# Attention scores by halves of their rows, q's norms by a diagonal and ones, single-row first tiles, first products of block 0 by kc

## The chip, the cores and the metric

The kernel runs on one core of a Trainium2 chip. The core has TensorE (PE, with its weight loads shown as PEld), VectorE (DVE), ScalarE (ACT), GpSimd (POOL) and SyncE (SP), each with a queue of its own that is worked off in order; DMA transfers are issued from the queues of SP and ACT. The metric is device time in microseconds, the median of several runs.

## What is computed

With N = 6016 tokens and C = 256 channels (B = 1); `moe_w_in` is 256 x 2048, `moe_w_out` 2048 x 256, and the second layer has the same shapes:

```python
qn = q / (np.linalg.norm(q, axis=1, keepdims=True) + 1e-06)
kn = k / (np.linalg.norm(k, axis=1, keepdims=True) + 1e-06)
s = kn.transpose(0, 2, 1) @ qn / tau          # 256 x 256
a = np.exp(s - s.max(-1, keepdims=True))
a /= a.sum(-1, keepdims=True) + 1e-09
x = v @ a
h = x @ w_in;   x = (h / (1 + np.exp(-1.702 * h))) @ w_out
h = x @ w2_in;  x = np.maximum(0.01 * h, h) @ w2_out
```

The weights come as float64 and are converted on the chip.

## The kernel before

**Front.** q and k are read in 15 tiles of 1, 1, 2, ten times 4, 2 and 1 rows of 128 tokens (`rows`, L318). `load_qk` issues q's transfer on SP and k's on ACT for the first three tiles and on SP after that, eight tiles ahead (`AHEAD`). For each tile PE forms the scores (L382): two products per row (kc = 0, 1), q's half as weights, k's row as moving operand, in full float32, so that each product is two instructions in the trace; all of them add up in two banks of PSUM (`s_ps`). ACT squares each tile and DVE adds the squares into `acc` (`add_squares`). Ahead of the last two tiles' scores PE forms the column sums of `acc` (`norms`, four products by `ones`, eight instructions). DVE and ACT make from them 1 / (norm + 1e-6); `dq` is a diagonal matrix of q's inverse norms over tau, `rk` holds k's as a scalar per row. ACT copies the scores to `st` (L436), four products by the diagonal (L442) scale them and bring them to the other orientation, and DVE takes each row's maximum (L450) for ACT's exponential (L455), which also adds up the denominators `den`. Four transposes (L463) turn the exponentials; `eth` and `etl` are their high and low parts (a float32 rounded to the one-pass format fp32r, and the rest).

**Splitting.** Every large product after the scores is three fp32r products, high by high, high by low and low by high (`terms`, L92). `halves` makes the two parts: a cast on ACT (L95) and a subtraction on DVE (L96).

**Fold.** Since x = v @ a is only used as x @ w_in, the attention is folded into the first weights: `fold(f)` multiplies `eth`/`etl` by the converted weight `wi` f (12 products of 256 columns), ACT scales by the denominators into `raw` (L490), DVE splits it into `wa[f]` (L496) and `raw` is stored to `w1raw[f]`. Fold 0 is made in the front, fold 1 within the hidden products of `f == NF`, the others in the loop over f.

**Block 0.** v's first 1024 tokens (two columns of blocks, u = 0, 1) are loaded into the buffer of q and k tile `V_TILE`, transposed by PE (`transpose_v`, eight transposes for each u, L410) and split into `xa[0]` (kc = 0) and `xbt` (kc = 1). For each of 8 weight tiles f and both halves s of the hidden units, `hidden_first` forms the hidden products of both u (12 instructions of 512 columns), ACT applies the gelu into `h` (one buffer, L514) and casts it to `gd` (L680), and DVE subtracts. `pend` holds finished hidden tiles; `emit_y(len(pend) - 2)` forms the output products y of the tiles before the last two, so y always lags one hidden tile behind.

**Weights.** `jobs` is a generator of small steps that convert a weight from float64: a scaling on ACT (L182), three integer steps on DVE (L203, L208, L212), a cast and a subtraction on DVE. `go_on(n)` puts the next n steps at the place where it is called; `next_load` issues the load of another weight on SP, at most three at a time. The order of weights is wi 0, wo 0, wi 1, wi 2, wo 1 and so on. The steps are called with 5 behind the scores of the second to last tile, 2, 2 and 4 in the rest of the front, and 4 and 2 in turn in block 0.

The rest of the kernel (blocks 1 to 5 of both layers, by seven products instead of eight) isn't touched. Within each engine, instructions run in the order in which the program emits them.

## Time and profile before

| | us |
|---|---|
| median of 3 runs (lowest, highest) | 1041.66 (1041.51, 1043.06) |
| the profiled execution | 1043.86 |
| its span | 1042.0 |
| PE busy | 1031.5 (99%) |
| DVE busy | 775.0 (74%) |
| ACT busy | 589.9 (57%) |

A page sums up one profiled execution. Its orders of time list, per engine, when a run of like instructions began, how long it lasted until the modelled end of the last, how many there were, and in brackets how long the engine had stood idle before and whom it then waited for. The granted clock is 1.00 at 2.4 GHz and 0.50 at 1.2 GHz.

### The profile page before, as it was taken

How to read it: one execution, taken by the hardware profiler on the slowest of the kernel's cores; microseconds unless marked ns; L12 is line 12 of the kernel's file. 1: busy time of each engine (PE TensorE's matmuls, PEld its weight loads, DVE VectorE, ACT ScalarE, POOL GpSimd, SP SyncE). 2: the span in 40 equal slices, each digit the busy share in tenths (PEclk: the TensorE clock that was granted, in tenths of full speed). 3: DMA queues.
4: the chain of work that ended last, by engine and by line, in shares of the span. 5: the costliest groups of instructions: out<-in, count | busy, mean ns of one | idle time of the engine just before them, and what ended most of it. 6: DMA issues, size and time to landing. Idle time of an engine off the chain costs nothing.

```text
span 1042.0 us, 12633 instructions
## 1 busy us (share of the span) xinstructions
PE 1031.5 (99%) x4676; PEld 870.6 (84%) x4676; DVE 775.0 (74%) x1187; ACT 589.9 (57%) x864; POOL 0.7 (0%) x7
## 2 busy tenths in 40 slices
PE   8999999999999999999999999999999999999998
PEld 7878888888888888888998888888888888888997
DVE  6889868888888888888766667577567667676655
ACT  5465555666556666666556555555555555455453
POOL 0000000000000000000000000000000000000000
PEclk9999999999999999999999999999999999999999
DMA  9646423015224223212744002101200300300202
GB/s 361 234 126 167 129 65 91 10 31 150 92 68 110 98 76 103 89 56 96 263 167 152 1 1 42 41 1 19 63 1 9 73 1 1 76 1 1 41 1 36
DMA packets 120077, 81.82 MB, mean 79 GB/s; under 512 B 93392, under 2 KB 104400, under 8 KB 118736
## 3 DMA queue, kind: packets, MB, share of 16 engines
q1 hardware_dynamic: 115872, 80.04, 25.3%
q10 hardware_dynamic: 4144, 0.98, 0.4%
q8 instruction: 36, 0.59, 0.2%
q14 instruction: 25, 0.20, 0.1%
HBM read 55.05 MB, written 25.95 MB: 78 GB/s over the span
## 4 chain that ended last, share of the span: by engine, by line
PE 97%; DVE 1%; DMA 1%; issue 0%; ACT 0%; ACTq 0%; DVEq 0%
PE y L92 49%; PE h L92 44%; PE y L382 4%; DMA qk<-in_k_dram 1%; DVE gd L99 0%; PE h L442 0%; ACTq L330 0%; ACT raw L490 0%; ACT sc L455 0%; DVE ta L208 0%; PE h L357 0%; DVE ta L203 0%; DVE etl L99 0%; DVE eth L467 0%; DVE ta L212 0%
## 5 line engine op out<-in xcount | busy, mean ns | idle before, releaser
L92 PE MATMUL y<-gd,wo 128*128 128x512 f32 (+1 forms) x1248 | 296.5, 386 | 0.1
L92 PE MATMUL h<-xa,wa 128*128 128x512 f32 (+1 forms) x1152 | 276.5, 385 | 0.5 <-DVE wa L496 0.5
L92 PEld LDWEIGHTS y<-gd,wo 128*128 128x128 f32 x1248 | 233.8, 188 | 44.1 <-DVE gd L99 0.4
L92 PEld LDWEIGHTS h<-xa,wa 128*128 128x128 f32 x1152 | 216.2, 188 | 41.7 <-DVE wa L496 0.8
L92 PE MATMUL y<-g,wo 128*128 128x512 f32 (+1 forms) x1044 | 246.8, 385 | 0.0
L92 PEld LDWEIGHTS y<-g,wo 128*128 128x128 f32 x1044 | 196.0, 188 | 36.3
L92 PE MATMUL h<-xb,wa 128*128 128x512 f32 (+1 forms) x888 | 217.3, 385 | 0.0
L92 PEld LDWEIGHTS h<-xb,wa 128*128 128x128 f32 x888 | 166.7, 188 | 31.1
L99 DVE TENSOR_TENSOR tv<-tp,h 128x512 f32<-128x512 f32 (+1 forms) x88 | 59.3, 674 | 114.4 <-PE h L92 111.8
L99 DVE TENSOR_TENSOR cc<-tv,h 128x512 f32<-128x512 f32 (+1 forms) x176 | 116.0, 673 | 34.9 <-PE h L92 34.4
L96 DVE TENSOR_TENSOR gd<-cc,gd 128x1024 fp32r<-128x1024 f32 (+1 forms) x87 | 104.1, 1197 | 0.0
L722 ACT COPY tp<-h 128x512 f32<-128x512 f32 (+1 forms) x87 | 50.4, 580 | 93.2 <-PE h L92 92.6
L95 ACT CAST gd<-cc 128x1024 fp32r<-128x1024 f32 (+1 forms) x87 | 90.0, 1035 | 0.0
L516 ACT ACTIVATE cc<-cc 128x1024 f32<-128x1024 f32 (+2 forms) x49 | 50.3, 1027 | 38.9 <-DVE cc L99 38.9
L516 ACT ACTIVATE tt<-tt 128x512 f32<-128x512 f32 (+1 forms) x48 | 30.0, 625 | 72.4 <-DVE tt L99 72.4
L99 DVE TENSOR_TENSOR tt<-tv,h 128x512 f32<-128x512 f32 (+1 forms) x88 | 59.4, 675 | 9.9 <-DVE tv L99 0.9
L99 DVE TENSOR_TENSOR tt<-tt,h 128x512 f32<-128x512 f32 (+1 forms) x88 | 59.4, 675 | 9.2
L514 ACT ACTIVATE cc<-cc 128x1024 f32<-128x1024 f32 (+1 forms) x40 | 41.6, 1041 | 40.9 <-DVE cc L99 40.9
L99 DVE TENSOR_TENSOR g<-tt,g 128x512 fp32r<-128x512 f32 (+1 forms) x87 | 58.6, 673 | 7.2 <-ACT g L733 6.9
L514 ACT ACTIVATE tt<-tt 128x512 f32<-128x512 f32 (+1 forms) x40 | 24.9, 623 | 64.8 <-DVE tt L99 64.8
L99 DVE TENSOR_TENSOR g<-tp,g 128x512 fp32r<-128x512 f32 (+1 forms) x87 | 58.6, 674 | 0.0
L746 ACT CAST g<-tp 128x512 fp32r<-128x512 f32 (+1 forms) x87 | 53.2, 612 | 2.8
(97 smaller groups left out, 713.0 us busy)
## 6 DMA issues: line engine op xcount, KB each, us to landing
cv<-in_moe_w_in_dram SPq DMA_DIRECT2D x32, 256.0 KB, 3.2
cv<-in_moe_w_out_dram SPq DMA_DIRECT2D x16, 512.0 KB, 3.9
wa<-w2a SPq DMA_DIRECT2D x8, 896.0 KB, 4.7
qk<-in_q_dram SPq DMA_DIRECT2D x10, 512.0 KB, 9.9
qk<-in_k_dram SPq DMA_DIRECT2D x10, 512.0 KB, 10.0
x<-stg SPq DMA_DIRECT2D x5, 1024.0 KB, 4.6
stg<-x SPq DMA_DIRECT2D x5, 1024.0 KB, 5.2
out_dram<-o SPq DMA_DIRECT2D x80, 64.0 KB, 1.9
```

The source lines that it names most:

```text
L92: nc.tensor.matmul(dst, lhsT=w, rhs=x, start=start, stop=stop, skip_group_check=more)
L95: nc.scalar.copy(hi, raw)
L96: nc.vector.tensor_tensor(out=lo, in0=raw, in1=hi.bitcast(F32), op=ALU.subtract)
L99: nc.vector.tensor_tensor(out=out, in0=in0, in1=in1, op=op)
L382: nc.tensor.matmul(s_ps[kc][:, :C], lhsT=t[:, 0, r, kc * P:(kc + 1) * P], rhs=t[:, 1, r, :], start=(j == 0 and r == 0), stop=(j == last an ...
L514: nc.scalar.activation(out=out, in_=in_, func=AF.Gelu_apprx_sigmoid)
L516: nc.scalar.activation(out=out, in_=in_, func=AF.Prelu, alpha=0.01)
L722: nc.scalar.copy(tp, pa)
L746: nc.scalar.copy(g11[:, 0], tp)
```

## The change

- The first tiles are six single rows, then 2, nine times 4, 2 and 1; k's loads of the first four go on ACT's queue. `ones` becomes 128 x 128 and is set before `ident`; the warm-up products use it.
- In the scores k's half is now the weight and q's row the moving operand, so that `s_ps[h]` holds 128 rows of k's channels by 256 of q's. For the last four tiles (11 rows) only half 0 is formed in the loop; half 1's 22 instructions are spread over what follows (`second_half`).
- The squares of the last three tiles are made for q and k apart, and the norms come behind all of half 0's scores.
- `st` and the four products by the diagonal go. `spread` multiplies the diagonal by `ones`, which gives q's inverse norms on every partition; ACT copies them to `rq`, and one `tensor_tensor_reduce` on DVE scales a half's scores and takes the row maxima.
- Softmax, turning, splitting and fold 0 are each done for one half h (or one kc) at a time, in an order written out by hand among transposes of v, scores and the kc = 0 part of the first hidden products (`first_products`).
- The casts of the high parts of `eth`, wi 0, wi 1 and wo 0 go from DVE to ACT.
- `V_TILE` becomes 10; one weight is loaded ahead of v and two behind it. The conversion steps in the front are 4, 1 and 5.
- For f = 0 the subtraction comes ahead of the four conversion steps, y of half s = 0 is not formed before the hidden products of s = 1, fold 1 comes between y of s = 0 and y of s = 1, and `pend` is emptied there.

`turn(h)` makes two transposes of `ex[:, h]` into bank h3; `fold_products` and `fold_scale` are the old loops of `fold` for one kc, with the high parts of `eth` first. Core of the diff:

```diff
-    ones = small(const, 1, "ones")
+    ones = const.tile([P, P], F32, name="ones")
...
+        nc.gpsimd.memset(ones, 1.0)
         make_identity(nc, ident)
-        nc.gpsimd.memset(ones, 1.0)
...
                 hi, lo = (wo[f][:, s].rearrange("p k c -> p (k c)") for s in range(2))
-                nc.vector.tensor_copy(hi, flat)
+                (nc.scalar.copy if f == 0 else nc.vector.tensor_copy)(hi, flat)
...
-                nc.vector.tensor_copy(wi[:, 0], flat)
+                (nc.scalar.copy if f < 2 else nc.vector.tensor_copy)(wi[:, 0], flat)
...
-        rows = [1, 1, 2] + [4] * 10 + [2, 1]
+        rows = [1] * 6 + [2] + [4] * 9 + [2, 1]
...
-                eng = nc.scalar if j < 3 and i == 1 else nc.sync
+                eng = nc.scalar if j < 4 and i == 1 else nc.sync
...
-        V_TILE = 7
-        CONVERT = {last - 1: 5}
+        V_TILE = 10
+        LATE = last - 3
...
+        def squares(j, i):
             t, n = qk(j), rows[j]
             sq = front.tile([P, 2, 4, C], F32, tag="sq", name="sq", bufs=2)
+            nc.scalar.activation(out=sq[:, i, :n, :], in_=t[:, i, :n, :], func=AF.Square)
+            for r in range(0, n, 2):
+                m = min(2, n - r)
+                add(acc[:, i, :m, :], acc[:, i, :m, :], sq[:, i, r:r + m, :])
+        def scores(j, halves_of, some=None):
+            t, n = qk(j), rows[j]
+            for r in range(n) if some is None else some:
+                for h in halves_of:
+                    nc.tensor.matmul(
+                        s_ps[h][:, :C],
+                        lhsT=t[:, 1, r, h * P:(h + 1) * P],
+                        rhs=t[:, 0, r, :],
+                        start=(j == 0 and r == 0),
+                        stop=(j == last and r == n - 1),
+                    )
...
+            scores(j, range(KC) if j < LATE else (0,))
...
             if j == V_TILE:
-                for _ in range(3):
-                    next_load()
+                next_load()
                 nc.sync.dma_start(out=taub, in_=tau.partition_broadcast(P))
                 for c in range(2):
                     nc.sync.dma_start(
                         out=qk(V_TILE)[:, c],
                         in_=v[c * BLK:(c + 1) * BLK, :].rearrange("(t p) c -> p t c", p=P),
                     )
+                for _ in range(2):
+                    next_load()
+        for j in range(LATE + 1, last + 1):
+            for i in range(2):
+                squares(j, i)
+        add(acc[:, :, 0, :], acc[:, :, 0, :], acc[:, :, 1, :])
+        for j in range(LATE + 1, last + 1):
+            scores(j, (0,))
+        go_on(4)
+        norms()
...
-        for d in range(KC):
-            nc.scalar.copy(st[:, d, :], s_ps[d][:, :C])
-        go_on(2)
-        sq_ps = [bank("h2"), bank("h3")]
-        for kc in range(KC):
-            for d in range(KC):
-                nc.tensor.matmul(
-                    sq_ps[kc][:, d * P:(d + 1) * P],
-                    lhsT=st[:, d, kc * P:(kc + 1) * P], rhs=dq[:, d, :], start=True, stop=True,
-                )
-        vt0 = transpose_v(0, ("y01", "y11"))
+        def spread():
+            nc.tensor.matmul(
+                nrm[:, C:2 * C], lhsT=ones, rhs=dq.rearrange("p k c -> p (k c)"),
+                start=True, stop=True,
+            )
+            nc.scalar.copy(rq, nrm[:, C:2 * C])
+        vt = {}
+        def transpose_v(kc, tags):
+            for u, tag in enumerate(tags):
+                vt[kc, u] = bank(tag)
+                for i in range(BLK // P):
+                    nc.tensor.transpose(
+                        vt[kc, u][:, i * P:(i + 1) * P],
+                        qk(V_TILE)[:, u, i, kc * P:(kc + 1) * P], ident,
+                    )
+        def split_v(kc, u):
+            dst = xbt if kc else xa[0]
+            halves(dst[:, 0, u], dst[:, 1, u], vt[kc, u])
+        def softmax(h):
+            nc.vector.tensor_tensor_reduce(
+                out=sc[:, h], in0=s_ps[h][:, :C], in1=rq, scale=rk[:, h:h + 1],
+                scalar=-3.0e38, op0=ALU.mult, op1=ALU.max, accum_out=mx[:, h:h + 1],
+            )
             nc.vector.tensor_scalar(
+                out=nmx[:, h:h + 1], in0=mx[:, h:h + 1], scalar1=-1.0, scalar2=None, op0=ALU.mult
             )
             nc.scalar.activation(
+                out=ex[:, h], in_=sc[:, h], func=AF.Exp, bias=nmx[:, h:h + 1],
+                scale=1.0, accum_out=den[:, h:h + 1],
             )
+        def split_e(h):
+            cols = slice(h * P, (h + 1) * P)
+            src = et[:, h * C:(h + 1) * C].rearrange("p (d c) -> p d c", d=KC)
+            nc.scalar.copy(eth[:, :, cols], src)
+            subtract(etl[:, :, cols], src, eth[:, :, cols].bitcast(F32))
+            nc.vector.tensor_scalar_add(rden[:, h:h + 1], den[:, h:h + 1], 1e-9)
+            nc.vector.reciprocal(out=rden[:, h:h + 1], in_=rden[:, h:h + 1])
...
+        def fold_half(raw, f, kc):
+            at = slice(0, 4, 3) if kc == 0 else slice(1, 3)
+            hi, lo = wa[f][:, 0, at], wa[f][:, 1, at]
+            nc.vector.tensor_copy(hi, raw[:, at])
+            subtract(lo, raw[:, at], hi.bitcast(F32))
+        late_rows = [(j, r) for j in range(LATE, last + 1) for r in range(rows[j])]
+        def second_half(count):
+            for j, r in late_rows[:count]:
+                scores(j, (1,), (r,))
+            del late_rows[:count]
+        transpose_v(0, ("h1", "h2"))
+        split_v(0, 0)
+        second_half(2)
+        spread()
+        go_on(1)
+        softmax(0)
+        split_v(0, 1)
+        second_half(4)
+        et = bank("h3")
+        turn(0)
+        split_e(0)
+        second_half(3)
+        wi0 = ready.pop(0)
+        raw0 = early.tile([P, 4, P], F32, tag="tp", name="raw")
+        pw0 = [bank(tag)[:, :C] for tag in ("y01", "y11")]
+        fold_products(pw0[0], wi0, 0)
+        second_half(len(late_rows))
+        transpose_v(1, ("y00", "h1"))
+        softmax(1)
+        fold_scale(raw0, pw0[0], 0)
+        fold_half(raw0, 0, 0)
+        hp0 = {}
+        def first_products(kc, pairs):
+            for s, u in pairs:
+                if kc == 0:
+                    hp0[s, u] = bank(f"h{2 * s + u}")
+                at = ((A11, A12), (A21, A22))[s][kc]
+                x = xbt if kc else xa[0]
+                terms(hp0[s, u], (wa[0][:, 0, at], wa[0][:, 1, at]), (x[:, 0, u], x[:, 1, u]),
+                      kc == 0, kc == KC - 1)
+        first_products(0, [(0, 0)])
+        turn(1)
+        split_e(1)
+        split_v(1, 0)
+        first_products(0, [(1, 0)])
+        fold_products(pw0[1], wi0, 1)
+        fold_scale(raw0, pw0[1], 1)
+        split_v(1, 1)
         nc.scalar.preload_act_table(AF.Gelu_apprx_sigmoid)
+        fold_half(raw0, 0, 1)
+        nc.sync.dma_start(out=w1raw[0], in_=raw0)
+        first_products(0, [(0, 1), (1, 1)])
+        go_on(5)
...
-                hp = bank(f"h{2 * s + u}")
-                for kc, x in enumerate((xa[0], xbt)):
-                    terms(hp, (wa[g][:, 0, at[kc]], wa[g][:, 1, at[kc]]),
-                          (x[:, 0, u], x[:, 1, u]), kc == 0, kc == KC - 1)
+                if g == 0:
+                    hp = hp0[s, u]
+                    first_products(1, [(s, u)])
+                else:
+                    hp = bank(f"h{2 * s + u}")
+                    for kc, x in enumerate((xa[0], xbt)):
+                        terms(hp, (wa[g][:, 0, at[kc]], wa[g][:, 1, at[kc]]),
+                              (x[:, 0, u], x[:, 1, u]), kc == 0, kc == KC - 1)
                 act(1, h[:, u], hp)
-            if f == NF:
-                fold(1)
             nc.scalar.copy(gd[:, 0], h)
-            if f < 2 * NF - 1:
+            if 0 < g and f < 2 * NF - 1:
                 go_on(4)
             subtract(gd[:, 1], h, gd[:, 0].bitcast(F32))
+            if g == 0:
+                go_on(4)
             for u in range(2):
                 pend.append((1, 0, u, f, gd[:, 0, u], gd[:, 1, u]))
@@ -698,7 +769,15 @@
                         go_on(1)
                     if f:
                         fold(f + 1)
-                emit_y(len(pend) - 2)
+                if f == 0 and s == 0:
+                    continue
+                if f == 0:
+                    emit_y(2)
+                    fold(1)
+                    emit_y(2)
+                    fetch()
+                else:
+                    emit_y(len(pend) - 2)
                 if f + 1 < NF or s == 0:
                     go_on(2)
                 fetch()
```

## Rows read from the trace of the kernel before

**Rows 1.** The page, its first part: busy time of each engine.
```profile
PE 1031.5 (99%) x4676; PEld 870.6 (84%) x4676; DVE 775.0 (74%) x1187; ACT 589.9 (57%) x864; POOL 0.7 (0%) x7
```

**Rows 2.** Order of time of PE (with PEld): start, length, instruction, [idle before, releaser].
```profile
1.35 2.93 PE L372 MATMUL h<-ident 128*128 128x128 f32 x12 [1.35 <-POOL ones L132]
4.07 2.53 PE L382 MATMUL y<-qk 128*128 128x256 f32 x8
8.85 38.16 PE L382 MATMUL y<-qk 128*128 128x256 f32 x168 [2.25 <-DMA qk<-in_k_dram]
46.84 0.95 PE L357 MATMUL h<-ones,acc 128*128 128x1 f32 x8
47.65 2.84 PE L382 MATMUL y<-qk 128*128 128x256 f32 x12
50.51 1.37 PE L442 MATMUL h<-dq,st 128*128 128x128 f32 x8
51.72 1.04 PE L410 MATMUL y<-ident,qk 128*128 128x128 f32 x8
52.95 1.02 PE L463 MATMUL h<-ident,sc 128*128 128x128 f32 x4 [0.20 <-ACT sc L455]
54.75 0.50 PE L92 MATMUL h<-wi,eth 128*128 128x256 f32 x2 [0.78 <-DVE eth L467]
...
58.32 1.22 PE L92 MATMUL h<-xa,wa 128*128 128x512 f32 x3 [0.52 <-DVE wa L496]
...
66.09 2.40 PEld L92 LDWEIGHTS y<-gd,wo 128*128 128x128 f32 x11 [0.41 <-DVE gd L99]
...
75.75 0.84 PE L92 MATMUL h<-xa,wa 128*128 128x512 f32 x3
```

**Rows 3.** Windows, the scores (L382) alone: PE busy, instructions, granted clock, DMA share, GB/s.
```profile
9.00:10.00 1.00, 1.00 (x3) 0.50 1.03 418
...
12.00:13.00 1.00, 1.00 (x6) 0.91 1.04 426
...
15.00:45.00 30.00, 30.00 (x141) 1.00 0.89 339
```

**Rows 4.** DMA issues by size (to landing), and a window with its GB/s at the end.
```profile
qk<-in_q_dram SPq DMA_DIRECT2D x3, 128.0 KB, 2.7
...
qk<-in_k_dram ACTq DMA_DIRECT2D x1, 256.0 KB, 7.1
...
3.00:3.50 0.50, 0.50 (x4) 0.50 (x4) 0.00 (x0) 0.49 (x2) 0.00 (x0) 1.00 1.34 359
```

**Rows 5.** Order of time of all engines: the last additions of 4-row squares.
```profile
33.90 5.07 DVE L99 TENSOR_TENSOR acc<-acc,sq 128x1024 f32<-128x1024 f32 x4
```

**Rows 6.** Order of time of DVE and ACT from the conversion to the first y.
```profile
42.46 0.69 DVE L208 SCALAR_TENSOR_TENSOR ta<-cv,ta 128x512 int32<-128x512 int32 x1
...
47.82 0.16 DVE L417 TENSOR_SCALAR rr<-h 128x4 f32<-128x4 f32 x1 [2.68 <-PE h L357]
...
49.15 0.60 DVE L427 TENSOR_SCALAR dq<-ident,rn,rtau 128x128 f32<-128x128 f32 x2
...
51.47 0.43 DVE L450 TENSOR_REDUCE mx<-h 128x1 f32<-128x256 f32 x1 [0.58 <-PE h L442]
...
52.24 0.56 ACT L455 ACTIVATE sc<-h,mx,rk 128x256 f32<-128x256 f32 x1 [1.35 <-DVE mx L451]
...
53.94 0.57 ACT L95 CAST xa<-y 128x512 fp32r<-128x512 f32 x1
...
55.02 1.28 ACT L473 ACT_TABLE_LOAD   x1
...
56.97 0.84 ACT L490 ACTIVATE raw<-h,rden 128x256 f32<-128x256 f32 x2 [0.67 <-PE h L92]
...
62.28 1.05 ACT L680 CAST gd<-h 128x1024 fp32r<-128x1024 f32 x1
...
64.82 1.22 DVE L99 TENSOR_TENSOR gd<-h,gd 128x1024 fp32r<-128x1024 f32 x1
```

More of the change, by code (lines that the diff above doesn't have):

```diff
@@ L371, in tile_kernel @@
         for _ in range(6):
[L372 to L373 removed]
+            nc.tensor.matmul(warm[:, :P], lhsT=ones, rhs=ones, start=True, stop=True)
+        for j in range(LATE + 1):
             t, n = qk(j), rows[j]
[L375 to L391 removed]
+            scores(j, range(KC) if j < LATE else (0,))
+            sq = front.tile([P, 2, 4, C], F32, tag="sq", name="sq", bufs=2)
+            nc.scalar.activation(out=sq[:, :, :n, :], in_=t[:, :, :n, :], func=AF.Square)
+            for r in range(0, n, 2):
+                m = min(2, n - r)
+                add(acc[:, :, :m, :], acc[:, :, :m, :], sq[:, :, r:r + m, :])
             if j + AHEAD <= last:
@@ new lines, in fold_products, with fold_scale @@
+        def fold_products(pw, f_wi, kc):
+            c0 = slice(kc * P, (kc + 1) * P)
+            wi = f_wi.rearrange("p h (d n) -> p h d n", d=KC)
+            todo = [(eth, 0, d) for d in range(KC)] + [(eth, 1, d) for d in range(KC)]
+            todo += [(etl, 0, d) for d in range(KC)]
+            for i, (e, x, d) in enumerate(todo):
+                nc.tensor.matmul(
+                    pw, lhsT=e[:, d, c0], rhs=wi[:, x, d], start=i == 0, stop=i == len(todo) - 1
+                )
+        def fold_scale(raw, pw, kc):
+            nc.scalar.activation(
+                out=raw[:, 0::3] if kc == 0 else raw[:, 1:3],
+                in_=pw.rearrange("p (s n) -> p s n", s=2), func=AF.Copy,
+                scale=rden[:, kc:kc + 1],
+            )
@@ L481, in fold @@
             pw = bank("h0" if f == 1 else "h3").rearrange("p (k n) -> p k n", k=KC)
             for kc in range(KC):
[L483 to L486 removed]
+                fold_products(pw[:, kc], wi, kc)
             raw = early.tile([P, 4, P], F32, tag="tp", name="raw")
             for kc in range(KC):
[L490 to L494 removed]
+                fold_scale(raw, pw[:, kc], kc)
@@ L498, in fold @@
             nc.sync.dma_start(out=w1raw[f], in_=raw)
-        fold(0)
-        vt1 = transpose_v(1, ("y00", "y10"))
-        for dst, src in ((xa[0], vt1[0]), (xbt, vt1[1])):
-            halves(dst[:, 0, 1], dst[:, 1, 1], src)
-        go_on(4)
         fctx.close()
```

85 lines of the change are left out of this document (11 added, 74 removed).

## Prediction

> **What bounds the kernel now.** I read the page's head first: PE is busy for 99% of the span, DVE for 74% [rows 1]. A change to the front can therefore gain only what PE waits for there, or does there and need not do. Next I read PE's order of time over the first 76 us [rows 2]. The reader is to see three things. The six warm-up products and the first two tiles of scores run from 1.35 to 6.60; then PE stands 2.25 us for tile 2's k; and the following 168 score instructions run without a break. The clock's windows [rows 3] show what the stop costs beyond itself: from 9 to 10 the granted clock is 0.50 (the 1.2 GHz level), from 12 to 13 it is 0.91 on the way back to 2.4 GHz, and from 15 to 45 there are 141 instructions in 30 us, 0.213 each. So some 3.3 us at half pace lost 1.65 more.
>
> Behind the scores come small stops: 0.20 before the turning of the exponentials and about 0.5 inside it (four transposes last 1.02, eight of v last 1.04), 0.78 before the fold, 0.52 before the first hidden product and 0.38 inside it (1.22 for three, 0.84 at 75.75), 0.41 before the first y [rows 2]. Taken together: from the norms (46.84) to 75.75, where y of both halves of block 0, fold 1, hidden 1 and fold 2 are done, 28.9 us pass. Their instructions at dense pace are 12 score instructions x 0.213, norms 0.81, diagonal 1.2, 20 transposes x 0.115, 36 fold products x 0.12 and 60 products of 512 columns x 0.227 (from 0.84 for three, of which one lasts 0.386): 24.8. So 4.1 us of stops. Behind 75.75 PE is dense; that part only moves.
>
> **Part 1, the six single-row tiles.** Now tile 2 brings two rows by two transfers of 256 KB, the k of which lands 7.1 us after its issue; single-row transfers of 128 KB land after 2.7 [rows 4]. After, rows 0 to 5 come singly, the k of the first four on ACT's queue; while such small packets moved, 359 GB/s were carried [rows 4], which is 0.73 us a row against the 0.85 that PE needs for its four instructions. With row 0 landed by 3.4, row 4 is there at 6.3, row 5 at 7.1, the 2-row tile at 8.5 and the first 4-row tile, at the 426 GB/s of the window from 12 to 13 [rows 3], at 11. PE: the `ones` are set before the identity, so the warm-up starts some 0.4 earlier and tile 0 at 3.6; its four instructions go at half pace (1.7), because the eight of now take 2.53 where 0.213 each would be 1.7 [rows 2]; then 162 at 0.213. That is 3.6 + 1.7 + 34.5 = 39.8, and 0.3 for one late tile: 166 instructions by 40.1. The present kernel has 176 by 46.84, so 166 by 44.7. Term 1 is **-4.6**. Ends: -5.0 with no tile late; -2.3 if a stop like today's 2.25 comes back at the 4-row tile.
>
> The rule that speaks against this stands in the Trainium skill, "DMA: Bandwidth & Descriptors", section "Rules for kernel authors": at least 1 MiB a transfer for full bandwidth, and many small ones put together. Rows agree in kind (359 GB/s against 426) but not in what matters here, landing time.
>
> The norms need the squares too. DVE adds four rows in 2 x 1.27 [rows 5]. Tile 7 can be added from some 13.0 (landed at 11, squared by ACT first), eight 4-row tiles take it to 33.6, and the late tiles, now squared q and k apart, add 2.4 + 1.2 + 0.7 and the merge 0.7: 38.7. PE comes later, so no term; but DVE then has the first weight's three steps (1.8, by 0.69 [rows 6]) to do in front of the norms' first step, and is done with them at 40.5: no slack is left.
>
> Moved in SP's queue: v's two loads now stand ahead of the loads of wo 0 and wi 1, not behind them. v is first needed behind the norms, and lands sooner; wo 0 and wi 1 land later by v's 1 MB, 2.4 us at that rate, and are first wanted by ACT's scaling behind the norms. Loads and their users lie some 5 us apart, so I cost both at nothing; if that cover is gone, the stops at the first y grow by what is missing. The store of `raw` 0 comes later and is read only when all the first weights are folded: nothing.
>
> **Part 2, the order behind the norms.** Removed: `st` copies and four products by the diagonal (eight instructions, 1.2). Added: one product of `ones` by it (two, 0.43). Term 2 is **-0.75**. The ten score instructions that move behind the norms cost the same there; what counts is whether this work covers the chains. I walk the four queues in issue order from the norms' end (R), with durations of rows 6. Steps without a row are set as follows. `tensor_tensor_reduce` on 256 elements: the reduction that it replaces takes 0.43, and a second pass for the multiplication would make it 0.86; it reads the same columns, so a gain is excluded; I take 0.5, near the reduction, and the other end puts 0.36 on each half's chain. Half casts and half scalings: 0.3 to 0.42 (`raw`: 0.84 for two).
> - `spread` waits for dq: 1.93 from rr to dq, 0.16 behind DVE's other work; cover is eight transposes and four score instructions. Stop 0.45.
> - turn of half 0: copy 0.42, DVE still in v's and the weight's subtractions, then 0.5 + 0.2, exponential and its sum 0.7; cover eight score instructions (1.7). Stop 1.0.
> - first hidden product: half 1's scores end at R + 8.4, then 0.5, 0.2, 0.7, `fold_scale` 0.42, cast 0.3; cover only eight transposes. Stop 1.5.
> - second pair of first products: its bank h1 is held by v's transposes until `split_v(1, 1)` is through, whose ACT cast is queued behind `fold_scale(1)`, which waits for the fold. Stop 1.9.
> - first y: ACT has the table load (1.28), a scaling and the cast of wo 0, which waits for three DVE steps, queued in front of the activations of the hidden products (0.6 each), the 1024-wide cast (1.05) and DVE's subtraction (1.22). Today a fold and hidden products for the other half lie between; now half of these are done already. Stops 1.1 and 1.0.
> - fold 1: wi 1's cast waits on ACT and DVE, 0.7. y of the other half is now issued at once: its activations wait for that cast and for the first subtraction (one buffer `h`), 0.9. Hidden 1: 0.4.
>
> Sum 9.0 against 4.1: term 3 is **+4.9**. Ends: if ACT's casts of the weights are out of the way in time, the last stops (1.1, 1.0, 0.7, 0.9) vanish and the sum is 5.3, so +1.2; if the thin stretch brings the 1.2 GHz level again, +1.7 more, so +6.6.
>
> **Sum.** -4.6 - 0.75 + 4.9 = -0.45. DVE and ACT do nearly the same work in the later stages, which therefore take as long. The profiled execution has a span of 1042.0 and 1043.86 in all; the median of the runs is 1041.66. I put the difference on the median: **1041.2**. The half-pace stretch of this execution need not be in each run of before; where it is absent, term 1 is smaller by up to 1.65.
>
> **The rivals.**
> (a) Cover holds: faster. The front's gain stays and ACT is ahead of the casts; the stops are 5.3 to 6. -4.6 - 0.75 + 1.2 to 1.9 = -3.5 to -4.2: 1037.5. For it: ACT is busy for 57% [rows 1], and the loads may be there early. Against it: the casts wait for DVE, not for ACT's time. It decides if PE stops for less than 1 us at the first y. Chance 0.31.
> (b) The thin stretch slows the clock: slower. Between the turn of half 1 and the first y, PE would have stops of 1.9, 1.1 and 1.0 with some 3 us of work among them. Today a stop of 2.25 behind a short run of work was followed by 0.50 [rows 2, 3]; the stops of 0.2 to 0.8 around 53 were not. It decides where a stop of some 2 us follows others: +1.7, and with term 1 at -3.5 the sum is +2.3: 1044.0. Chance 0.14.
> (c) The loads don't come earlier: the 4-row tile lands late and the stop of 2.25 comes back, with or without the half pace. Term 1 is -2.3, or less, and the sum +1.9 or more: 1043.8. The page's rule on small transfers would bring it out so. Chance 0.10.
> (d) My forecast, within 0.2%: 0.45.
>
> **How the numbers follow.** The bound of 0.2% (2.1 us) is about what a measurement of this kernel can tell from no change. Faster is (a), 0.31; slower is (b) and (c), 0.24; the rest 0.45. The low end takes -5.0, -0.75 and +1.2: -4.5, 1037.2. The high end takes -2.3, -0.75 and +6.6: +3.5, 1045.2; I cut it to 1044.6, since (b) and (c) together are rare. The forecast's own range is 1039.6 to 1043.7.
>
> **What would show it.** Part 1: no PE stop over 1 us before the norms, weight loads at full pace from some 5 us on, norms at 39.5 to 41. Wrong if a wait on `qk` over 1 us stands there. Part 2: stops in the places and sizes above, named by the chain's rows `ex`, `raw`, `xb`, `gd`; wrong if the first y starts under 20 us after the norms' end (rival a), or if the clock's column shows 0.5 between 45 and 70 (rival b). Later: PE dense from about 72, and phases of equal length.

## The result, and the profile after

| | before | after |
|---|---|---|
| median of 4 runs (lowest, highest), us | 1042.2 (1041.51, 1043.06) | 1048.23 (1046.98, 1049.48) |
| the profiled execution | 1043.86 | 1046.98 |
| its span | 1042.0 | 1045.2 |

The ratio after to before is 1.0057, with an interval of 1.004 to 1.0075: the changed kernel is slower by 6.0 us, outside the range that I gave. Each run also lists its span and the mean granted clock of that span. Where this mean is 0.999 or 1.0, which I call "at full clock" from here on, the medians of one kernel's spans lie close together: 1040.15 to 1040.3 for before in four series (its single runs from 1039.0 to 1041.1), 1045.2 and 1045.6 for after. The other two runs of after, at 0.998, have 1047.3 and 1047.7. So there are two losses: 5.2 us that every run has, and some 2.1 more in the runs in which the clock fell.

The page of after, its first part, answers [rows 1]. The busy time of PE is the same to 0.1 us:

```profile
PE 1031.4 (99%) x4670; PEld 869.2 (83%) x4670; DVE 774.5 (74%) x1195; ACT 593.6 (57%) x874; POOL 0.8 (0%) x7
```

PE's order of time over the front and block 0's first weight tile, with the columns of [rows 2]:

```profile
0.99 2.93 PE L382 MATMUL h<-ones 128*128 128x128 f32 x12 [0.99 <-POOL ones L131]
3.71 7.09 PE L355 MATMUL y<-qk 128*128 128x256 f32 x24
11.20 1.97 PE L355 MATMUL y<-qk 128*128 128x256 f32 x8 [0.40 <-DMA qk<-in_k_dram]
14.05 29.16 PE L355 MATMUL y<-qk 128*128 128x256 f32 x134 [0.88 <-DMA qk<-in_k_dram]
43.04 0.95 PE L367 MATMUL h<-ones,acc 128*128 128x1 f32 x8
43.85 1.07 PE L445 MATMUL h<-ident,qk 128*128 128x128 f32 x8
44.76 1.03 PE L355 MATMUL y<-qk 128*128 128x256 f32 x4
47.12 0.70 PE L433 MATMUL h<-dq,ones 128*128 128x256 f32 x2 [1.33 <-DVE dq L424]
47.66 1.89 PE L355 MATMUL y<-qk 128*128 128x256 f32 x8
49.64 0.44 PE L470 MATMUL h<-ident,ex 128*128 128x128 f32 x2
...
55.03 0.97 PE L92 MATMUL h<-xa,wa 128*128 128x512 f32 x3 [1.22 <-DVE wa L502]
...
59.53 1.62 PE L92 MATMUL h<-xa,wa 128*128 128x512 f32 x6 [1.86 <-DVE xb L96]
60.99 2.88 PE L92 MATMUL h<-xb,wa 128*128 128x512 f32 x12
64.61 0.50 PE L92 MATMUL y<-gd,wo 128*128 128x512 f32 x1 [0.73 <-ACT gd L749]
65.87 2.81 PE L92 MATMUL y<-gd,wo 128*128 128x512 f32 x11 [0.76 <-DVE gd L99]
68.51 1.02 PE L488 MATMUL h<-wi,eth 128*128 128x256 f32 x4
...
71.63 2.83 PE L92 MATMUL y<-gd,wo 128*128 128x512 f32 x11 [0.76 <-DVE gd L99]
...
78.87 0.86 PE L92 MATMUL h<-xa,wa 128*128 128x512 f32 x3
```

The reader is to see three things. First, the scores: the long stop of [rows 2] is split in two (0.40 and 0.88), and yet the norms stand at 43.04 where I had 40.1. Second, every stop behind the norms waits for something that DVE or ACT has yet to make: `dq`, `wa`, `xb`, `gd`. In brackets they are 6.66 us; in [rows 2] the brackets of the same stretch hold about 1.9. Third, PE is dense from 82 us on, as it was before from 76.

The windows of the first 13 us, all instructions (columns: PE, PEld, DVE, ACT, POOL busy, granted clock, DMA share, GB/s), answer [rows 3]:

```profile
2.00:10.00 8.00, 8.00 (x32) 6.96 (x31) 4.15 (x6) 4.96 (x7) 0.00 (x0) 1.00 0.92 281
7.00:8.00 1.00, 1.00 (x5) 0.85 (x5) 0.90 (x2) 0.93 (x2) 0.00 (x0) 1.00 0.74 175
...
12.00:13.00 1.00, 1.00 (x6) 0.69 (x4) 0.74 (x1) 0.23 (x1) 0.00 (x0) 1.00 1.04 422
```

PE alone shows what its first score instructions cost: 3 or 4 in each us up to 7, and 6 in the us from 8 to 9. From 3.71 to 7.19 they start 0.43 us apart, from there on 0.215 (columns: PE busy, granted clock, DMA share, GB/s).

```profile
4.00:5.00 1.00, 1.00 (x3) 1.00 0.88 267
5.00:6.00 1.00, 1.00 (x4) 1.00 0.93 295
6.00:7.00 1.00, 1.00 (x4) 1.00 1.00 315
...
8.00:9.00 1.00, 1.00 (x6) 1.00 1.17 299
```

The same window of before, 2 to 10 us, carried 331 GB/s:

```profile
2.00:10.00 8.00, 5.75 (x22) 4.82 (x22) 1.42 (x3) 3.60 (x4) 0.00 (x0) 0.92 0.96 331
```

And the DMA issues of after in these 8 us by size, with the median time to landing, which answer [rows 4]:

```profile
qk<-in_k_dram ACTq DMA_DIRECT2D x2, 128.0 KB, 4.3
qk<-in_k_dram SPq DMA_DIRECT2D x2, 128.0 KB, 3.2
...
qk<-in_k_dram SPq DMA_DIRECT2D x1, 256.0 KB, 4.8
```

A transfer of 128 KB that took 2.7 in [rows 4] takes 3.2 to 4.3 here, and from 7 to 8 us only 175 GB/s move.

When the loads are issued stands in SP's own order of time. In before, q of tile 3, its first 4-row tile, is the last of the four q loads from 0.73 on, and k follows at 2.59:

```profile
0.73 1.82 SPq L330 DMA_DIRECT2D qk<-in_q_dram  x4
2.59 0.43 SPq L330 DMA_DIRECT2D qk<-in_k_dram  x1
```

In after the two loads of its first 4-row tile, tile 7, are issued at 6.78 and 7.25:

```profile
6.78 0.43 SPq L330 DMA_DIRECT2D qk<-in_q_dram  x1
7.25 0.43 SPq L330 DMA_DIRECT2D qk<-in_k_dram  x1
```

In both kernels the first eight loads of q and k are issued without a wait for a landing. The ninth waits until one of them has landed, and so on with each later one: in after it is issued at 3.60, and the first scores, which need the same landing, start at 3.71.

DVE and ACT ahead of the norms and behind them, in order of time, answer [rows 5] and [rows 6]:

```profile
15.96 25.81 DVE L99 TENSOR_TENSOR acc<-acc,sq 128x1024 f32<-128x1024 f32 x24 [2.47 <-ACT sq L387]
41.80 0.69 DVE L99 TENSOR_TENSOR acc<-acc 128x512 f32<-128x512 f32 x1
42.41 0.42 DVE L203 TENSOR_SCALAR ta<-cv 128x512 int32<-128x512 int32 x1
42.94 0.69 DVE L208 SCALAR_TENSOR_TENSOR ta<-cv,ta 128x512 int32<-128x512 int32 x1
43.67 0.69 DVE L212 SCALAR_TENSOR_TENSOR ta<-cv,ta 128x512 int32<-128x512 int32 x1
...
44.35 0.14 DVE L414 TENSOR_SCALAR rr<-h 128x4 f32<-128x4 f32 x1
44.39 0.62 ACT L231 CAST wi<-ta 128x512 fp32r<-128x512 f32 x1 [1.39 <-DVE ta L212]
...
44.92 0.20 ACT L415 ACTIVATE root<-rr 128x4 f32<-128x4 f32 x1
...
46.46 0.60 DVE L424 TENSOR_SCALAR dq<-ident,rn,rtau 128x128 f32<-128x128 f32 x2 [0.53 <-DVE rn L422]
```

DVE starts on the first 4-row tile at 15.96, adds with no stop that the profile names until 42.4 and then has the three steps of the first weight, so it is a second path of nearly the same length as PE's: had PE been done at 40.1, the norms would have had to wait for `acc` until 42.4.

### The profile page after: what moved, and what is told of

Same layout as the page of the kernel before. It is cut to its first block, busy times and chain, and to the rows that moved or that the text cites. A ratio compares the mean times of both kernels' runs of the same rounds, so it can differ in the third digit from the quotient of the medians.

```text
span 1045.2 us, 12652 instructions
## 1 busy us (share of the span) xinstructions
PE 1031.4 (99%) x4670; PEld 869.2 (83%) x4670; DVE 774.5 (74%) x1195; ACT 593.6 (57%) x874; POOL 0.8 (0%) x7
## 4 chain that ended last, share of the span: by engine, by line
PE 92%; DVE 4%; DMA 1%; ACT 1%; issue 1%; SPq 0%; ACTq 0%; DVEq 0%
PE y L92 49%; PE h L92 43%; DVE acc L99 2%; DMA qk<-in_k_dram 1%; PE h L488 1%; DVE ta L208 0%; DVE ta L212 0%; DMA xr<-in_v_dram 0%; SPq L666 0%; ACT h L581 0%; PE y L355 0%; ACT gd L749 0%; ACT sq L387 0%; DVE ta L203 0%; PE y L488 0%
## 5 line engine op out<-in xcount | busy, mean ns | idle before, releaser
L99 DVE TENSOR_TENSOR cc<-tv,h 128x512 f32<-128x512 f32 (+1 forms) x176 | 115.8, 672 | 35.8 <-PE h L92 35.5
```

Of the source, the lines that this page charges most:

```text
L99: nc.vector.tensor_tensor(out=out, in0=in0, in1=in1, op=op)
```

## The experiments

Each was run beside the kernel before on the same chip. The last column is the median span of the runs at full clock, with their number; the series of before have 1040.15 to 1040.3 there.

| | edit | median, us | ratio to before | full clock |
|---|---|---|---|---|
| after | | 1048.23 | 1.0057 [1.004, 1.0075] | 1045.4 (2 of 4) |
| e1 | before, six single-row tiles | 1042.54 | 1.0008 [0.9999, 1.0016] | 1040.6 (5 of 11) |
| e2 | after, tiles of before | 1047.78 | 1.0051 [1.0038, 1.0063] | 1045.8 (4 of 5) |
| e3 | after, casts on DVE | 1046.99 | 1.0044 [1.0032, 1.0057] | none of 5 |
| e4 | after, block 0 of before | 1047.37 | 1.0053 [1.0039, 1.0067] | 1045.0 (1 of 5) |
| e5 | before, six fillers | 1042.0 | 0.9999 [0.9991, 1.0008] | 1040.1 (10 of 11) |
| e6 | before with `spread` | 1042.88 | 1.0005 [0.9996, 1.0014] | 1040.2 (1 of 11) |
| e7 | e6 and e5's fillers | 1042.81 | 1.0003 [0.9994, 1.0012] | 1040.4 (3 of 11) |
| e8 | before, tiles 1, 1, 1, 1, 2, 2, 4 | 1040.99 | 0.9986 [0.9977, 0.9995] | 1038.95 (8 of 10) |
| e9 | e6 with e8's tiles | 1042.34 | 1.0004 [0.9996, 1.0013] | 1039.6 (5 of 11) |
| e10 | e9 with fillers | 1041.7 | 0.9995 [0.9986, 1.0004] | 1039.5 (7 of 11) |
| e11 | e3 with fillers | 1045.92 | 1.0038 [1.0025, 1.005] | 1044.05 (4 of 5) |
| e12 | after with fillers | 1047.58 | 1.0051 [1.0037, 1.0065] | 1045.7 (5 of 5) |
| e13 | e6, conversion steps moved | 1041.94 | 0.999 [0.9981, 0.9999] | 1039.4 (8 of 11) |
| e14 | e13 with e8's tiles | 1040.88 | 0.9991 [0.9981, 1.0] | 1038.6 (7 of 11) |

### Which part loses: e1 and e2

e1 is before with nothing but part 1's tiles; e2 is after with the tiles, the queue and `V_TILE` of before. The edit of e1, which e2 has the other way round:

```diff
-        rows = [1, 1, 2] + [4] * 10 + [2, 1]
+        rows = [1] * 6 + [2] + [4] * 9 + [2, 1]
-                eng = nc.scalar if j < 3 and i == 1 else nc.sync
+                eng = nc.scalar if j < 4 and i == 1 else nc.sync
-        V_TILE = 7
+        V_TILE = 10
```

> The kernel before with only the six single-row first tiles (k of four of them on ACT's queue, v in the buffer of tile 10). Theory A, the first tiles gain nothing because the rows that have landed by 11 us are eight either way and PE is bound by their landing: within 1 us of before (ratio 0.999 to 1.001), the 4-row tile's k landing at 13.5 to 14.5, a PE stop of 0.5 to 1.5 in front of it. Theory B, the small transfers cost time of their own: 2 to 4 us slower (ratio 1.002 to 1.004). The prediction's term (4.6 us earlier) would give 0.996.

> The changed kernel with the first tiles of before (1, 1, 2, then 4 rows; k of three on ACT's queue, v in the buffer of tile 7); everything behind is as changed. Theory A, the new order behind the norms costs what its stops add (35.8 us against 28.9 from the norms to the end of fold 2, of which 2.1 are score products that moved): 4 to 5.5 us slower than before (ratio 1.004 to 1.0055), as slow as the whole change or nearly. Theory B: at most 1.5 us slower (1.0015), the rest of the loss being the tiles'.

e1 made no difference that can be told, e2 has the whole loss: part 1 as it stands is worth nothing, and the order costs 5.5 us at full clock. PE's order of time of e1:

```profile
6.34 5.45 PE L382 MATMUL y<-qk 128*128 128x256 f32 x24 [0.28 <-DMA qk<-in_k_dram]
14.36 33.01 PE L382 MATMUL y<-qk 128*128 128x256 f32 x144 [2.57 <-DMA qk<-in_k_dram]
47.21 0.95 PE L357 MATMUL h<-ones,acc 128*128 128x1 f32 x8
```

The stop of before is back, at the first 4-row tile and as long as ever, and with it the fall of the clock (window 10 to 20):

```profile
10.00:20.00 10.00, 7.43 (x27) 5.91 (x26) 4.93 (x5) 5.25 (x4) 0.00 (x0) 0.83 0.98 367
```

And e2, with the same 166 score instructions ahead of its norms as after, in an execution whose clock did not fall:

```profile
8.53 34.53 PE L355 MATMUL y<-qk 128*128 128x256 f32 x158 [2.82 <-DMA qk<-in_k_dram]
42.89 0.95 PE L367 MATMUL h<-ones,acc 128*128 128x1 f32 x8
...
46.57 0.70 PE L433 MATMUL h<-dq,ones 128*128 128x256 f32 x2 [0.93 <-DVE dq L424]
```

With the old tiles the norms stand at 42.89, with the new ones at 43.04. One stop of 2.82 early on costs no more than eight instructions at half pace and two shorter stops, because the rows that have landed by then are as many: in before, tile 3's k landed at 11.1 us and made eight rows; in after, the eighth row came with tile 6's k, also at 11.1, and the twelfth row came at 13.6 and 13.9.

### Which of the order: e3 and e4

e3 gives the high parts of wi 0, wi 1 and wo 0 back to DVE; e4 gives block 0's first weight tile the order of before.

```diff
-                (nc.scalar.copy if f == 0 else nc.vector.tensor_copy)(hi, flat)
+                nc.vector.tensor_copy(hi, flat)
-                (nc.scalar.copy if f < 2 else nc.vector.tensor_copy)(wi[:, 0], flat)
+                nc.vector.tensor_copy(wi[:, 0], flat)
```

```diff
+            if f == NF:
+                fold(1)
...
-            if 0 < g and f < 2 * NF - 1:
+            if f < 2 * NF - 1:
                 go_on(4)
...
-                if f == 0 and s == 0:
-                    continue
-                if f == 0:
-                    emit_y(2)
-                    fold(1)
-                    emit_y(2)
-                    fetch()
-                else:
-                    emit_y(len(pend) - 2)
+                emit_y(len(pend) - 2)
```

> The changed kernel with the casts of wi 0, wi 1 and wo 0 back on DVE. Theory A, the activations of the first hidden products are held up by those casts in ACT's queue: the first y starts about 0.5 to 1 us sooner after the norms and the kernel is 0.5 to 1.5 us faster than the changed one (ratio to before 1.0042 to 1.0052). Rival, DVE is what the subtractions wait for, and has 1.3 us more to do: no faster, up to 1 us slower (1.0057 to 1.0067).

> The changed kernel with block 0 ordered as in the kernel before: fold 1 ahead of the first y, y one hidden tile behind, the conversion steps ahead of the first subtraction. Theory A, giving up the distance between a hidden product and its y is what costs 2 to 2.5 of the stops (0.7 and 0.8 at the first y, 0.8 at the second, and fold 1's wait): 1.5 to 2.5 us faster than the changed kernel (ratio to before 1.0033 to 1.0043). Rival, the chain of activation, cast and subtraction is the same and the conversion steps now stand in front of it: within 0.7 us of the changed kernel (1.005 to 1.0064).

Neither brings the time of before back. e4 is as slow as after: fold 1 now waits 1.47 for `wi`, a new stop for the ones that went. The clock fell in four of its five runs (0.83 from 60 to 70 us in the profiled one), so what its order is worth at full clock rests on a single run, 1045.0. In e3 the stop ahead of the first y falls from 0.73 to 0.27 and the one of the other half is gone; but in all of its five runs the clock fell. Twelve products that take 2.88 in after take 4.26, where the window shows 0.83:

```profile
61.48 4.26 PE L92 MATMUL h<-xb,wa 128*128 128x512 f32 x12
```

```profile
60.00:70.00 10.00, 8.97 (x31) 6.62 (x31) 7.01 (x12) 6.41 (x10) 0.00 (x0) 0.83 0.18 53
```

What the casts are worth is therefore hidden here, at least in part, behind what the clock took.

### The clock by itself: e5, e11 and e12

Products of `ident` by `ident` into a bank that nothing reads keep PE at work in its stops. e5 puts six behind tile 1 of before, in the stop of 2.25; e11 and e12 put twelve into the stops of e3 and of after (4 ahead of the first hidden product, 6 ahead of the second pair, 2 ahead of the first y):

```diff
+            if j == 2:
+                for _ in range(6):
+                    nc.tensor.matmul(warm[:, :P], lhsT=ident, rhs=ident, start=True, stop=True)
```

```diff
+        idle = bank("y10")
+        def fill(count):
+            for _ in range(count):
+                nc.tensor.matmul(idle[:, :P], lhsT=ident, rhs=ident, start=True, stop=True)
+        fill(4)
         first_products(0, [(0, 0)])
...
+        fill(6)
         first_products(0, [(0, 1), (1, 1)])
...
+                    fill(2)
                     emit_y(2)
```

> The kernel before with six more products of the identity (their result is not used) behind the scores of tile 1, where PE stands 2.25 us for tile 2's k. Theory A, that stop lets the clock fall to 1.2 GHz in part of the executions, at 1.65 us each: with the filler the granted clock stays at 1.00 from 5 to 20 us and the median is 0.5 to 1.5 us below before (ratio 0.9985 to 0.9995). Rival, the fall is not due to that stop, or the filler runs past tile 2's landing: 1.000 to 1.001, with 0.5 still to be seen in the clock's column.

> The changed kernel with the casts on DVE (e3) and twelve filler products in its stops: four before the first hidden product, six before the second pair of first products, two before the first y. Theory A: e3 lost one fall of the clock, some 1.7 us, in every run; with the fillers the clock stays up and the median is 1044.8 to 1045.8 (ratio 1.0025 to 1.0035), the rest of the loss being the stops themselves. Rival, the clock is not what e3 lost: 1046.5 to 1047.5 (1.0042 to 1.005).

> The changed kernel with the same twelve filler products and its casts on ACT. Theory A: its runs all end as its undisturbed ones, 1046.8 to 1047.6 (ratio 1.0045 to 1.0053), so that the stops cost about 5 us at full clock, and the casts on ACT some 2 of them by comparison with the last kernel. Rival, the stops are harmless at full clock: below 1045.

In e11 and e12 the fillers do what they are for: all five runs of e12 are at full clock, and four of e11's where e3 had none (in e11's profiled execution the clock fell behind the stop in front of the first 4-row tile, which has no filler). Their time at full clock is that of after (1045.7 against 1045.4), so they cost little in the stops. That separates the two losses: filled stops give back what the clock took in some runs, and leave 5.2 to 5.6. The pair also gives the price of the casts on ACT, 1045.7 - 1044.05 = 1.65. In e5 the front kept its clock (norms at 45.20, not the 46.84 of [rows 2], the 1.65 that I worked out from [rows 3]). But in the same execution it fell later, between 54 and 58 us:

```profile
50.00:60.00 10.00, 8.66 (x46) 7.10 (x45) 8.00 (x18) 7.22 (x14) 0.00 (x0) 0.83 0.26 79
```

The order there is that of before, and the stops ahead of the fall are the 0.20 and 0.78 of [rows 2] and 0.22 inside the fold. Ten of e5's eleven runs are at full clock, against 21 of the 33 of before in that series; its median is nevertheless that of before, since most runs of before had nothing to get back. The stretch at half pace on which I had spent a paragraph is thus no property of the kernel: it comes in some executions, and not always at the same place.

### The diagonal by ones, by itself: e6, e7, e13

e6 is before with the turned scores and `spread`: norms one tile earlier, then the last tiles' scores as the cover; softmax, turning and fold are left whole, as before. e7 adds e5's fillers.

```diff
-            if j == last - 1:
-                for i in range(last - 1, last + 1):
+            if j == last - 2:
+                for i in range(last - 2, last + 1):
                     add_squares(i)
                 norms()
+                go_on(3)
+                inverse()
+                go_on(2)
+            if j == last - 1:
+                spread()
+                for h in range(KC):
+                    for i in range(last - 1, last + 1):
+                        scores(i, (h,))
...
+            nc.vector.tensor_tensor_reduce(
+                out=sc[:, kc], in0=s_ps[kc][:, :C], in1=rq, scale=rk[:, kc:kc + 1],
+                scalar=-3.0e38, op0=ALU.mult, op1=ALU.max, accum_out=mx[:, kc:kc + 1],
+            )
...
         go_on(2)
...
         go_on(2)
         et = bank("h1")
```

> The kernel before with the scores turned, q's norms spread by the diagonal and ones and one pass of scaling and maximum, as in the change, but with the norms and their chain one 4-row tile earlier, all scores ahead of the softmax, and the cover of before: whole hidden products, no half folds, y one tile behind. Theory A, the loss lies in the cover that the change gives away and not in this step: the exponentials begin 0.9 to 1.4 us earlier after the last score (1.75 in before), one product of 0.43 stands for 1.2, and the kernel is 1 to 2 us faster than before (ratio 0.998 to 0.999). Rival, the turned scores or the new pass cost time themselves: 1.000 to 1.002.

> The last two kernels' edits together: turned scores with q's norms by the diagonal and ones and the cover of before, and the six filler products behind tile 1. Theory A: their gains add, 1.5 to 3.5 us faster than before (ratio 0.9967 to 0.9985). Rival: as either alone, or 1.000.

Both came out level with before, and the reason was my own edit: its two `go_on(2)`, the first of which stands ahead of the diagonal's products in before, now both stand on DVE ahead of the high part of the exponentials, the first of fold's waits grew from the 0.78 of [rows 2] to 1.78, and the clock fell in ten runs of eleven. The fillers of e7 stand at tile 2 and not in this stop; its clock fell in eight of eleven. PE's order of time of e6:

```profile
51.96 0.80 PE L92 MATMUL h<-wi,eth 128*128 128x256 f32 x2 [1.78 <-DVE eth L478]
```

e13 moves two of these four steps into DVE's idle time ahead of the first maximum and two behind the splitting of v:

```diff
                 spread()
+                go_on(2)
...
-        go_on(2)
-        go_on(2)
         et = bank("h1")
...
             halves(dst[:, 0, 0], dst[:, 1, 0], src)
+        go_on(2)
```

> The order of e6 (turned scores, norms by the diagonal and ones one tile earlier, whole softmax and fold as before), with the conversion steps of wo 0 moved: two into the idle time of DVE ahead of the first TENSOR_TENSOR_REDUCE (2.14 us in e6), two behind the splitting of v, none ahead of the high part of the exponentials. In e6 eth waited 1.78 on DVE. Theory: the spread is worth what I forecast and e6 lost it to these steps: fold starts 1.0 to 1.2 earlier, no stop over 0.9 ahead of it, clock fall gone; span at full clock 1039.2, median 1041.2, ratio 0.999. Rival: the spread has no gain of its own (the additions to the diagonal's wait at norms and the exchange of the bank cost as much), span at full clock 1040.2 as in e6, and ratio 1.000 or above.

The wait is back at its old 0.78,

```profile
52.16 0.50 PE L92 MATMUL h<-wi,eth 128*128 128x256 f32 x2 [0.78 <-DVE eth L477]
```

eight of eleven runs are at full clock, and their span is 1039.4 where before has 1040.2: -0.8. The idea of part 2 without the halving is a small gain, together with the norms one tile earlier, which e13 needs for its cover.

### The tiles once more: e8, e9, e10, e14

e8 is before with a milder front: four single rows and two tiles of two, k of the first four on ACT's queue.

```diff
-        rows = [1, 1, 2] + [4] * 10 + [2, 1]
+        rows = [1] * 4 + [2] * 2 + [4] * 9 + [2, 1]
-                eng = nc.scalar if j < 3 and i == 1 else nc.sync
+                eng = nc.scalar if j < 4 and i == 1 else nc.sync
-        V_TILE = 7
+        V_TILE = 9
```

e9 has these tiles in e6, e14 in e13; e10 is e9 with four fillers between the turning and the fold.

> The kernel before with first tiles of 1, 1, 1, 1, 2, 2 rows, then 4 (k of four on ACT's queue, v in the buffer of tile 9). Theory A, what has landed by 11 us is eight rows however they are cut, and twelve by 13.6 to 14: within 1 us of before (0.999 to 1.001), tile 6 (four rows, the ninth to the twelfth) landing at 13.5 to 14.5. Rival, the single rows of the change are too small and 2-row tiles land sooner: tile 6 by 12.5, and 1 us or more faster (below 0.999).

> The kernel before with first tiles of 1, 1, 1, 1, 2, 2 rows and, as in e6, the scores turned and q's norms by the diagonal and ones with the cover of before. Theory A (the front is shorter, but its softmax stretch has grown thin enough for the clock to fall in nearly every execution): clock 0.997 or 0.998 in most runs, median 1040.5 to 1041.5, no faster than the tiles alone (0.9986). Rival, the two gains add: below 1040.3 (ratio 0.998).

> The last kernel with four filler products of the identity (result not used) where PE stands in the softmax stretch: one between the two turnings, two before the fold, one before the first hidden product. Theory A: the clock stays up (1.00 from 45 to 65 us, 0.999 or 1.0 over the run), so that the stretch's gain is kept: median 1038.8 to 1040 (ratio 0.9966 to 0.998). Rival, the fillers only delay what waits behind them, or the clock falls all the same: 1040.5 to 1042.

> e13 with the first tiles of e8 (1, 1, 1, 1, 2, 2 rows). e8 alone had 1040.99 and spans of 1039.0 at full clock; e9 (e6 with these tiles) 1042.34, with norms that waited 1.04 on DVE's additions and a clock fall. Theory that the gains add up where DVE has room: span at full clock 1038.6, ratio 0.998. Rival that DVE is the bound ahead of the fold once the scores end earlier (norms wait again 1.0): span 1039.4, and ratio 0.9995, behind e8 alone.

e8 is faster than before by 0.14% (interval 0.9977 to 0.9995), and so beats both kernels. The stop is shorter, not gone:

```profile
13.82 31.32 PE L382 MATMUL y<-qk 128*128 128x256 f32 x144 [1.49 <-DMA qk<-in_k_dram]
44.98 0.95 PE L357 MATMUL h<-ones,acc 128*128 128x1 f32 x8
```

Its norms come only 0.2 ahead of e5's 45.20, but its span at full clock is 1.15 below e5's. The two profiles can't tell where the rest arises: e8's execution, 1039.7, is its longest at full clock, and e5's has the fall at 54 us, which made the next products some 0.6 later than e8's. e14 has 1038.6 at full clock, the shortest of all, so most of the two gains add up; but its norms wait for DVE again,

```profile
41.61 1.02 PE L358 MATMUL h<-ones,acc 128*128 128x1 f32 x8 [0.78 <-DVE acc L99]
```

and its clock fell in four runs of eleven, so that its ratio is no better than e8's. e9 and e10 (norms behind `acc` by 1.04 and 1.00) say the same. The four fillers of e10 did not do what I expected of them: its clock fell in four of eleven runs, in the profiled one at 55 us, behind the largest stop left (1.32), and its median is 1041.7 where I had 1038.8 to 1040.

## Why the prediction was wrong, point by point

The result is slower by 6.0 us where I put -0.45. At full clock, where the clock's share is out of the comparison, the parts come out so:

| | forecast | measured | from |
|---|---|---|---|
| term 1, tiles | -4.6 (-5.0 to -2.3) | +0.3 or -0.4 | e1 against before, after against e2 |
| term 2, `spread` | -0.75 | -0.8 | e13 against before |
| term 3, order | +4.9 (+1.2 to +6.6) | +6.3 | e2 against before, less term 2 |
| sum | -0.45 | +5.2 | after against before |
| clock (rival b) | +1.7, chance 0.14 | +2.1 in two runs of four | after's runs |

**Term 1 is the step that failed**: "the 2-row tile at 8.5 and the first 4-row tile ... at 11". PE could start on them at 11.20 and 14.05. I had divided bytes by a rate, as if every load stood ready behind the one before. They did not: with at most eight loads in flight, four single rows are 1024 KB where the first eight loads of before are 2048 KB, and all that follows is issued only as these land. The first 4-row tile's k was issued at 7.25 instead of 2.59 and took 6.7 us more. From 2 to 10 us 2.25 MB moved where before moved 2.65. A small transfer also takes longer than its bytes: 128 KB at 359 GB/s is 0.37 us, and the transfers of this size in [rows 4] took 2.7. I had this row and used it for row 0 alone. How much of the other 2.3 is a cost of each transfer and how much the bytes of the others in flight, no run separates, and none changed the number in flight. So the rows behind the small tiles came later by what the small tiles had gained, which is rival (c) in its first sentence, at a chance of 0.10. The Trainium skill, "DMA: Bandwidth & Descriptors", section "Anatomy of one DMA — SWDGE (gpsimd) path", gives a fixed 2.0 us for each transfer of GpSimd's path besides the bytes. The loads here are issued by SP and ACT, so no run of this case tests that figure. The rule in the same page of the Trainium skill, section "Rules for kernel authors", on 1 MiB a transfer and on putting small ones together, which I had set aside because the rates agreed "in kind", pointed the right way: 281 GB/s from 2 to 10 us here, against 331 with the larger loads of before.

There was a second bound that I had worked out and not followed: DVE's additions. They are 0.64 us a row, take 26 us from the first 4-row tile on, and start 2 us behind its landing, when ACT has squared it. My 38.7 for their end (the parts that I named add up to 38.3) rested on the same landing at 11; with 14.0 it became 42.4. The price of a late tile was thus on two engines, and my end of -2.3 for "a stop like today's" had only one of them. The half pace at the start lasted for eight score instructions where I had four; these 0.85 us went into the wait for the 2-row tile. And the comparison itself was against a disturbed execution: 44.7 for 166 instructions held 1.65 us of half pace, which I had named and left in the sum. Of the -4.6, 1.65 was that and 2.95 the landing.

**Term 2 was right in size**: the products took 1.2 in [rows 2] and 0.54 in after, from 47.12 to 47.66. The -0.8 of e13 is near the forecast's -0.75, but e13 also has the norms earlier and other stops, so part of this agreement is luck. The sizes without a row held too: `tensor_tensor_reduce` took 0.48 and 0.08 for its read-out, where I had 0.5.

**Term 3 was right in kind and 1.4 too small.** From the norms to the end of fold 2 after needs 78.87 - 43.04 = 35.8; my walk gives 28.9 + 2.1 (the ten score instructions that moved) - 0.75 + 4.9 = 35.2. Its stops one by one:

| | forecast | bracket in after |
|---|---|---|
| `spread` | 0.45 | 1.33 |
| turn of half 0 | 1.0 | none |
| first hidden product | 1.5 | 1.22 |
| second pair of first products | 1.9 | 1.86 |
| first y | 1.1 + 1.0 | 0.73 + 0.76 |
| fold 1 | 0.7 | none |
| y of the other half | 0.9 | 0.76 |
| hidden 1 | 0.4 | none |

Places and names agree (`dq`, `wa`, `xb`, `gd`), and `xb`, held by a cast that is queued behind `fold_scale(1)`, is right to 0.04. `spread` was wrong because DVE's three steps of wi 0 ran until 44.28, in front of the norms' first step, and ACT's cast of wi 0 then held `root` until 44.92: the "no slack is left" of part 1 was spent. DVE then stood 0.53 more ahead of `dq`, for which I know no reason; in e2, where this is absent, the stop is 0.93. The brackets add up to less than my sum, and the stretch is longer all the same. Dense, its instructions would take 24.8 + 2.1 - 0.75 = 26.15 of the 35.8, so some 9.7 are lost and not 6.66: a bracket counts only from the modelled end of the last instruction, and some work between the stops runs below dense pace, as the four fold products in 1.02 at 68.51 and the three hidden ones in 0.97 at 55.03, where dense ones take 0.64 and 0.84. I had counted these losses as stops, which is why the total held. The walk's other 0.6 and what comes until 82 make up most of the rest of the 6.3.

**The rivals.** (a) is out: the first y stood 20.6 behind the norms' end, and although its stops stayed under the 1 us that I had set as the sign, the front's gain that (a) needs was not there. (b) came true in two of the four runs, at a price near mine (2.1 against 1.7). In the profiled execution of after the clock did not fall, so where it fell in the two is not shown; e3 and e4 show the fall behind the same stops of 1.2 and 1.9, from 60 us on, and e11 and e12 that products in these stops keep it off. I had its chance too low because I asked for stops near 2 us, and the other leg of my argument, that the stops of 0.2 to 0.8 around 53 bring no fall, held for one execution only: in e5 they were followed by one. (c) came true, with a front that gains nothing. The forecast (d) needed the front's gain, and without it its own terms 2 and 3 say +4.15, close to the 5.2 that every run has.

**What the halving costs, and what stays open.** The casts on ACT are 1.65 of the 6.3. The rest, some 4.6, the runs do not split further. e13 has `spread` without the halves and the casts, and 6.0 us less, but its norms are also one tile earlier and its `spread` does not wait, where in after it waits 1.33. Block 0's order seems to be worth little, by the one run of e4 at full clock. That the halves of softmax, turning and fold are the larger part of the 4.6 is therefore argued and not shown. Which of the stops would have to go was not tried one by one.

## What to carry to other kernels

Before work is cut into halves, compare what covers each half with the chain through the other engines; here the new order turned four stops of 0.2 to 0.8 us into six of 0.7 to 1.9, though each engine was as busy as before. Before a first load is made smaller, look in the queue's own rows when the loads behind it are issued and what they wait for; price a load by the landing time of its likes with as many in flight, not by bytes over a rate, and follow the late tile on every engine that reads it. Before a stop's pace is put into a sum, look whether each run has it: one filled stop (e5) or the spread of the spans by granted clock tells.

## What the runs showed of the hardware

- Transfers of 128 KB landed 2.7 us after their issue in before and 3.2 to 4.3 in after, where the first twelve loads are all of this size; the front made of them moved 281 GB/s from 2 to 10 us, against 331 with larger ones. In both kernels no more than eight loads of q and k were in flight, so that smaller ones meant fewer bytes on the way.
- The granted clock fell to the 1.2 GHz level behind stops of 1.2 to 1.9 us (e3, e4), behind one of 1.8 (e6) and behind smaller ones of 0.2 to 0.8 (e5), and in some executions of one kernel only: two of four for after, all five for e3, ten of eleven for e6, one of eleven for e5. With twelve products of 128 columns in the stops it stayed at 2.4 GHz in all five runs of e12 and four of e11's five; with four in e10, in seven of eleven.
- From 2 to 10 us of after the clock's column shows 1.00, yet the first eight score instructions start 0.43 us apart, twice the 0.215 of the next sixteen, with no stop among them. The trace has no record of the granted clock before 7.16 us, where the pace changes; in before the first record is at 5.35, and there too the starts go from 0.43 to 0.22 apart. A 1.00 at the very start of these traces is therefore not a reading.
